# First head pair scored from unsplit float32 operands, and the planner's table retuned, in a top-k attention with a rational feed-forward

## The chip, the cores and the metric

One Trainium2 chip, one core of it. The time is device microseconds of that core for one execution; smaller is better. The engines are named as the profile names them: PE (TensorE; PEld is its weight load), DVE (VectorE), ACT (ScalarE), POOL (GpSimd) and SP (SyncE, whose queue issues every DMA of this kernel).

## The reference

```python
# attention: 8 batches, 8 heads, 576 rows, head size 64
scores = scale * np.matmul(q, k.transpose(0, 1, 3, 2))
kth = np.partition(scores, -top_k, axis=-1)[..., -top_k:-top_k + 1]     # top_k = 32
mask = scores >= kth
scores = np.where(mask, scores, -1000000000.0)
scores = scores - np.max(scores, axis=-1, keepdims=True)
attn = np.exp(scores)
attn = attn / (np.sum(attn, axis=-1, keepdims=True) + 1e-09)
attn_out = np.matmul(attn, v)
# feed-forward on x = attn_out, 4608 tokens by 512, inner size 2048
h = x @ w_in
P = a[0] + a[1] * h + a[2] * h2 + a[3] * h3                              # h2 = h*h, h3 = h2*h
Q = 1.0 + np.abs(b[0]) * np.abs(h) + np.abs(b[1]) * h2
g = P / (Q + 1e-06)
out = (g @ w_out)
```

## The kernel before, in words

**Attention.** Heads go in pairs: two heads of 64 channels fill the 128 partitions. For each batch and pair, 512 of the 576 query rows make four units of 128 rows, with one tile for each head of the pair (128 queries by 576 keys); the last 64 rows of both heads make one "mixed" tile. That is 288 tiles. A tile is scored on PE into PSUM (`scores`, L693; mixed tiles L690), copied to SBUF by ACT (`evacuate`, L700), and then DVE does the selection: it folds the two halves of 288 keys into a maximum `hi` and a minimum `lo` (L711, L704), picks eight at a time with MAX8 (L722) and MATCH_REPLACE8 (L730) until it has the 32nd largest, and multiplies mask and exponentials (`probs`, L764). ACT makes the exponentials (L761). PE turns the result (`trp`, L841), ACT copies it out (`p`, L853), PE multiplies with the values (`av`, L867). The reciprocal of the row sum is widened to 128 columns (`widen`, `rw`, on POOL L287 or ACT L285), turned by PE beside the third piece of the probabilities (L843), evacuated with it into the buffer `p2`, and multiplied into the result on POOL (`x_m`, L886).

**Split operands.** PE runs most products on fp32r operands. To keep float32 accuracy, a float32 operand is split into a high part (a copy rounded to fp32r) and a low part (the difference), and products are summed. For queries and keys that is a chain: DMA of `kl` and `qx`, a high copy (L279 on ACT or L281 on POOL), a subtraction on POOL (L592, L635), then DMAs that stack high and low parts of one head over the partitions (`ka`, `kb` L601, `q` L642 and L644). A tile then takes four fp32r matmuls of 288 columns. The mixed tiles skip all of this: they multiply float32 operands as they come (`km`), two matmuls a tile.

**Feed-forward.** A chunk of 256 tokens goes through eight groups: 24 matmuls `ph` (L1014), the rational function on ACT and POOL, and 12 matmuls `po` (L1160); chunks begin when their attention is done. Weights arrive as 64-bit floats, and 64 half-blocks are turned into float32: two operations on ACT (L416, L421), a bit merge on DVE (L427), one on ACT (L433), a product on POOL (L437), then the split (L279 or L281, L453). Before the first group, a chain of one-column operations works out the coefficients: blocks on POOL (L482, L484) with reciprocals on DVE between them (L488) and one closing operation on DVE (L552).

**Order.** Nothing is scheduled at run time. A planner (`Plan`) runs over all steps with estimated lengths, keys (smaller goes first) and rings of buffers (`ROOM`), and writes out one fixed order for each engine; on the chip an engine stops at an instruction until its semaphores are there, and all behind it waits. The dictionary `KEY` holds keys, engine choices and ring sizes; `later=` adds an estimated delay to the point at which a step may be planned. A slow full version of the program follows behind a branch and is not executed here.

Of the kernel before, what the change touches and what calls it, by code (L numbers as in the profile page):

```python
# [644 lines left out]

# [733 lines left out]
```

## Time and profile before

| | us |
|---|---|
| median of 3 runs (1514.39 to 1516.71) | 1515.34 |
| profiled execution | 1513.21 |
| its span | 1511.1 |
| PE busy in the span | 1391.7 (92%) |
| DVE busy | 1356.2 (90%) |
| ACT busy | 1270.4 (84%) |
| POOL busy | 1213.7 (80%) |

The profiled execution lies 2.1 us below the median and 2.1 us above its own span. Shares of busy time are means over stages: early on PE has little to do, and at the end DVE has nothing.

### The profile page before, as it was taken

How to read it: one execution, taken by the hardware profiler on the slowest of the kernel's cores; microseconds unless marked ns; L12 is line 12 of the kernel's file. 1: busy time of each engine (PE TensorE's matmuls, PEld its weight loads, DVE VectorE, ACT ScalarE, POOL GpSimd, SP SyncE). 2: the span in 40 equal slices, each digit the busy share in tenths (PEclk: the TensorE clock that was granted, in tenths of full speed). 3: DMA queues.
4: the chain of work that ended last, by engine and by line, in shares of the span. 5: the costliest groups of instructions: out<-in, count | busy, mean ns of one | idle time of the engine just before them, and what ended most of it. 6: DMA issues, size and time to landing. Idle time of an engine off the chain costs nothing.

```text
span 1511.1 us, 32498 instructions
## 1 busy us (share of the span) xinstructions
PE 1391.7 (92%) x9729; PEld 1174.3 (78%) x9729; DVE 1356.2 (90%) x4567; ACT 1270.4 (84%) x2512; POOL 1213.7 (80%) x1862
## 2 busy tenths in 40 slices
PE   2556789999999899999999999999999999999998
PEld 1334567878888788888888888888888788888886
DVE  5889999999999999999999999999999999999200
ACT  5768989988888788988888988888888699889774
POOL 5987898887877688887977888787878688878896
PEclk9667799999999999999999999999999999999999
DMA  8757876657765767567756776667665776564564
GB/s 240 217 176 232 236 243 207 186 158 226 231 200 153 236 200 229 176 204 214 232 175 188 221 235 202 181 189 220 207 205 156 225 208 211 157 196 148 162 203 139
DMA packets 175226, 303.21 MB, mean 201 GB/s; under 512 B 26304, under 2 KB 80576, under 8 KB 175040
## 3 DMA queue, kind: packets, MB, share of 16 engines
q1 hardware_dynamic: 175040, 301.03, 65.0%
q8 instruction: 80, 1.31, 0.4%
q14 instruction: 106, 0.87, 0.2%
HBM read 229.64 MB, written 18.87 MB: 164 GB/s over the span
## 4 chain that ended last, share of the span: by engine, by line
PE 68%; DMA 8%; POOL 6%; DVE 6%; ACT 5%; SPq 4%; issue 2%; POOLq 0%; ACTq 0%; DVEq 0%
PE ph_m L1014 19%; PE po_m L1160 18%; PE av L867 10%; PE s L693 7%; PE trp L841 7%; PE ph_t L1014 3%; DMA wi_m<-win_l 3%; PE po_t L1160 2%; DVE m L722 2%; DVE hi L730 2%; PE s L690 1%; SPq L644 1%; DMA wl_m<-wout_l 1%; DMA w_w<-in_moe_w_in_dram 1%; DVE pr L764 1%
## 5 line engine op out<-in xcount | busy, mean ns | idle before, releaser
L722 DVE MAX8 m<-hi 128x8 f32<-128x288 f32 (+1 forms) x1152 | 502.9, 455 | 0.2
L730 DVE MATCH_REPLACE8 hi<-m,hi 128x288 f32<-128x288 f32 x864 | 381.2, 446 | 0.0
L1014 PE MATMUL ph_m<-xh_m,win_h 128*128 128x256 f32 x1024 | 305.9, 299 | 2.9 <-ACT p L853 2.9
L1014 PE MATMUL ph_m<-xh_m,wi_m 128*128 128x256 f32 x1024 | 289.3, 283 | 8.3 <-DMA wi_m<-win_l 8.0
L1014 PE MATMUL ph_m<-xl_m,win_h 128*128 128x256 f32 x1024 | 288.2, 281 | 0.0
L853 ACT COPY p<-trp 128x512 f32<-128x512 f32 (+1 forms) x448 | 227.5, 513 | 37.1 <-PE trp L841 20.5
L841 PE MATMUL trp<-ident,pr 128*128 128x128 f32 x1312 | 223.2, 282 | 37.7 <-ACT w_w L433 23.5
L761 ACT ACTIVATE e<-sb,st 128x576 f32<-128x576 f32 x288 | 216.7, 752 | 26.5 <-DVE pr L764 17.1
L700 ACT COPY sb<-s 128x576 f32<-128x576 f32 x288 | 185.0, 642 | 61.2 <-PE s L693 51.0
L764 DVE SCALAR_TENSOR_TENSOR pr<-sb,m,e 128x576 f32<-128x576 f32 x288 | 230.7, 801 | 0.8 <-ACT e L761 0.7
L841 PEld LDWEIGHTS trp<-ident,pr 128*128 128x128 f32 x1312 | 163.5, 144 | 70.4 <-ACT w_w L433 28.9
L1070 POOL TENSOR_TENSOR pa_m<-pa_m,va_m 128x512 f32<-128x512 f32 x128 | 165.2, 1292 | 65.7 <-ACT va_m L1067 61.6
L1160 PE MATMUL po_m<-wout,g_m 128*128 128x512 f32 x512 | 217.5, 425 | 0.0
L1160 PE MATMUL po_m<-wl_m,g_m 128*128 128x512 f32 x512 | 203.7, 398 | 4.3 <-DMA wl_m<-wout_l 4.3
L1160 PE MATMUL po_m<-wout,gl_m 128*128 128x512 f32 x512 | 202.6, 396 | 1.1 <-DMA q<-qx 0.7
L1014 PEld LDWEIGHTS ph_m<-xh_m,wi_m 128*128 128x128 f32 x1024 | 193.2, 189 | 10.8 <-DMA wi_m<-win_l 10.7
L1014 PEld LDWEIGHTS ph_m<-xh_m,win_h 128*128 128x128 f32 x1024 | 193.5, 189 | 9.9 <-ACT p L853 4.5
L867 PE MATMUL av<-p,vm 128*64 128x256 f32 (+1 forms) x1920 | 187.6, 344 | 9.2 <-ACT w_w L433 6.0
L1014 PEld LDWEIGHTS ph_m<-xl_m,win_h 128*128 128x128 f32 x1024 | 193.6, 189 | 2.2
L1089 POOL TENSOR_TENSOR pa_m<-pa_m,hh_m 128x512 f32<-128x512 f32 x128 | 165.5, 1293 | 15.2 <-ACT hh_m L1095 5.3
L867 PEld LDWEIGHTS av<-p,vm 128*64 128x64 f32 x1920 | 111.9, 142 | 77.5 <-issue 16.0
L1076 POOL TENSOR_TENSOR gl_m<-pa_m,g_m 128x512 fp32r<-128x512 f32 x128 | 165.9, 1297 | 4.6 <-PE po_t L1160 0.2
(120 smaller groups left out, 3211.7 us busy)
## 6 DMA issues: line engine op xcount, KB each, us to landing
wl_m<-wout_l SPq DMA_DIRECT2D x256, 256.0 KB, 3.6
wi_m<-win_l SPq DMA_DIRECT2D x128, 512.0 KB, 4.2
vm<-in_v_dram SPq DMA_DIRECT2D x96, 320.0 KB, 3.2
q<-qx SPq DMA_DIRECT2D x128, 128.0 KB, 2.8
q<-qx SPq DMA_DIRECT2D x256, 64.0 KB, 2.2
km<-in_qk_dram SPq DMA_DIRECT2D x32, 352.0 KB, 3.7
kl<-in_qk_dram SPq DMA_DIRECT2D x32, 288.0 KB, 3.9
qx<-in_qk_dram SPq DMA_DIRECT2D x64, 128.0 KB, 3.5
```

Of the source, the lines that this page charges most:

```text
L700: nc.scalar.copy(t.sb, t.s[:, :, 0:HF])
L722: nc.vector.max(to, t.both if not full and o == 24 else getattr(t, src))
L730: nc.vector.match_replace(x, t.m[:, o : o + 8], x, NEG)
L761: nc.scalar.activation(t.e, t.sb, AF.Exp, scale=SCALE, bias=t.st)
L764: nc.vector.scalar_tensor_tensor(out=t.pr, in0=t.sb, scalar=t.kth, in1=t.e, op0=ALU.is_ge, op1=ALU.mult, accum_out=u.ss[:, t.h : t.h + 1],)
L841: nc.tensor.transpose(u.ps[i][:, c * P : (c + 1) * P], u.pr[:, x], ident)
L853: nc.scalar.copy(pair.pT[i][:, at].rearrange("p c n -> p (c n)"), u.ps[i][:, 0 : n * P])
L867: nc.tensor.matmul(pair.av[d, 0 : u.nq * len(pair.units)], lhs, x[:, 0, d] if u.mixed else x[:, 0] if lone else x, start=(c == 0), stop=(c ...
L1014: nc.tensor.matmul(y.ph[:, f * NT : (f + 1) * NT], w, z[:, c, :], start=(c == 0 and i == 0), stop=(c == HP - 1 and i == 2),)
L1076: engine().tensor_tensor(out=tile_("gl", F32R), in0=y.pa, in1=y.g.bitcast(F32), op=ALU.subtract)
L1089: nc.gpsimd.tensor_tensor(out=x, in0=x, in1=z, op=ALU.mult)
L1160: nc.tensor.matmul(o.po[i], z, w, start=(ff == 0 and n == 0), stop=(ff == NF - 1 and n == 2),)
```

## The change

Four things change.

1. For the first head pair of the first batch (`index == 0`), keys and queries are loaded once as float32 and multiplied as they are: one plain DMA each in place of load, split and stacking, and two float32 matmuls a tile in place of four fp32r ones, for its eight tiles. Each matmul uses the 64 partitions of its head.
2. The loads of the mixed operands of the first batch get a key that is 14 tiles later.
3. The planner takes 0.32 us in place of 0.19 us for one coefficient operation on POOL, and holds a bit merge 0.431 us longer (`ML`).
4. Entries of `KEY`: `XH` (high copies of x, keys, queries) from POOL or ACT to POOL alone; `WD` (widening) from POOL or ACT to ACT alone; `PJ` (key of `po`) 92.472 to 101.114; `RI` (key of the first denominator step) 11.198 to 7.085; rings `p2` 2 to 1, `m` 2 to 3, `ob` 3 to 4; `IL` 1.0 to 0.996, `GL` 0.3 to 0.285.

```diff
@@ -440,7 +440,7 @@

                 s1 = add("ACT", act_sb(256), sign, [ld], key + 1)
                 s2 = add("ACT", act(256, 1), ends3, [ld], key + 1, take=[bits_hold])
-                s3 = add("DVE", 0.36, merge, [s1, s2], key + 1)
+                s3 = add("DVE", 0.36, merge, [s1, s2], key + 1, later=KEY['ML'])
                 s4 = add("ACT", act_sb(256), size, [s3], key + 2, give=[bits_hold])
                 last.append(
                     add("POOL", pool_t(256), join, [s4], key + 2, give=hold if plain else [])
@@ -482,7 +482,7 @@
                         nc.gpsimd.tensor_scalar(o, x, s1, 0.0, op0=op0, op1=ALU.add)
                     else:
                         nc.gpsimd.tensor_scalar(o, x, s1, s2, op0=op0, op1=op1)
-            to("POOL", 0.19 * len(ops), emit)
+            to("POOL", 0.32 * len(ops), emit)

         def over(o, x):
             to("DVE", 0.16, lambda: nc.vector.reciprocal(o, x))
@@ -579,6 +579,11 @@
         kv.index, kv.nm = index, nm
         kv.khold, kv.mhold = Hold("k", 2 * NJ), Hold("km")
         rhold = Hold("kr")
+        kv.plain = index == 0
+
+        def load_plain():
+            kv.x = buf(kv.khold, [P, S], F32, f"ka_{nm}", "a")
+            nc.sync.dma_start(kv.x, qk[index][:, 0:S])

         def load():
             kv.low = buf(rhold, [P, S], F32, f"kl_{nm}", "l")
@@ -607,11 +612,15 @@
             kv.km, kv.qm = x[:, 0:S], x[:, S:]

         k2 = key + KEY['KL']
+        kv.mload = add("SP", dma(1, P * (S + P)), load_mixed, key=key + KEY['QL'] + (14 * T if bi == 0 else 0),
+                       take=[kv.mhold])
+        if kv.plain:
+            kv.load = add("SP", dma(1, P * S), load_plain, key=k2, take=[kv.khold])
+            return kv
         ld = add("SP", dma(1, P * S), load, key=k2, take=[rhold])
         s = add(one(S, 0, KEY['XH']), None, high_part, [ld], k2 + 1, later=KEY['LD'])
         s = add(two(S, *KEY['LP']), None, low_part, [s], k2 + 1)
         kv.load = add("SP", 4 * dma(1, D * S), stack, [s], k2 + 2, take=[kv.khold], give=[rhold])
-        kv.mload = add("SP", dma(1, P * (S + P)), load_mixed, key=key + KEY['QL'], take=[kv.mhold])
         return kv

 
@@ -622,6 +631,10 @@
         nm = f"{kv.nm}_{u.j}"
         q = pair.q = Obj()
         q.hold, rhold = Hold("q", 2 * len(pair.units)), Hold("qr")
+
+        def load_plain():
+            q.x = buf(q.hold, [P, 2, 2, 2 * P], F32, f"q_{nm}")[:, 0, 0]
+            nc.sync.dma_start(q.x[:, 0:n], qk[kv.index][:, S + u.j * P :][:, 0:n])

         def load():
             q.x = buf(rhold, [P, 2, 2 * P], F32R, f"qx_{nm}")
@@ -643,6 +656,9 @@
                 for i in range(2):
                     nc.sync.dma_start(x[there, i, h, 0:n], y[here, 1 - i, 0:n])

+        if kv.plain:
+            q.load = add("SP", dma(1, P * n), load_plain, key=key + KEY['QL'], take=[q.hold])
+            return
         ld = add("SP", dma(1, P * n), load, key=key + KEY['QL'], take=[rhold])
         s = add(one(n, 0, KEY['XH']), None, high_part, [ld], key + KEY['QL'] + 1, later=KEY['LD'])
         s = add(two(n, *KEY['LP']), None, low_part, [s], key + KEY['QL'] + 1)
@@ -683,13 +699,19 @@

         def scores():
             t.s = s = bank("s", [P, 2, 512], f"s_{t.nm}")
-            for i in range(1 if u.mixed else 2):
+            for i in range(1 if u.mixed or kv.plain else 2):
                 for hf in range(2):
                     cols = slice(hf * HF, (hf + 1) * HF)
                     if u.mixed:
                         nc.tensor.matmul(s[:, hf, 0:HF], kv.qm, kv.km[:, cols], start=True, stop=True)
                         continue
                     o = (u.j - u.pair.units[0].j) * P
+                    if kv.plain:
+                        d = slice(t.h * D, (t.h + 1) * D)
+                        nc.tensor.matmul(
+                            s[:, hf, 0:HF], u.pair.q.x[d, o : o + P], kv.x[d, cols], start=True, stop=True
+                        )
+                        continue
                     nc.tensor.matmul(
                         s[:, hf, 0:HF], u.pair.q.q[:, i, t.h, o : o + P], kv.k[t.h][:, cols],
                         start=(i == 0), stop=(i == 1),
@@ -770,8 +792,8 @@
             s = add("PE", 2 * pe_f(HF), scores, [kv.mload, prev.s], key - 3.2, take=[shold],
                     give=[kv.mhold], crit=True)
         else:
-            s = add("PE", 4 * pe_r(HF), scores, [kv.load, u.pair.q.load, prev.s], key - 3.2, take=[shold],
-                    give=[kv.khold, u.pair.q.hold], crit=True, kind="r")
+            s = add("PE", 2 * pe_f(HF) if kv.plain else 4 * pe_r(HF), scores, [kv.load, u.pair.q.load, prev.s], key - 3.2, take=[shold],
+                    give=[kv.khold, u.pair.q.hold], crit=True, kind="f" if kv.plain else "r")
         prev.s = s
         e = add("ACT", act(S), evacuate, [s], key - 2.6, take=[sbhold], give=[shold], crit=True)
         fhi = add("DVE", dve(HF), fold_hi, [e, u.fold], key - 0.6, take=[hihold] if t.h == 0 else [], give=[shold])
```

Every order is written anew by the planner. Three places of it follow; where a line's number differs between the programs, the first is before.

**SP, from the start of the program.** `km` are mixed operands, `qx` and `kl` the queries and keys to be split, `vm` values, `w_w` weight halves. Before:

```order
L606 DMA km_0_127<-in_qk_dram 128x704
L628 DMA qx_0_0_129<-in_qk_dram 128x256
L585 DMA kl_0_131<-in_qk_dram 128x576
L658 DMA vm_0_0_133<-in_v_dram 128x640
L368 DMA w_w_0_135<-in_moe_w_in_dram 128x512
L368 DMA w_w_1_137<-in_moe_w_in_dram 128x512
L606 DMA km_1_142<-in_qk_dram 128x704
L642 DMA q_0_0_146<-qx_0_0_129 64x2x256
L644 DMA q_0_0_146<-qx_0_0_129 64x256 x2
L642 DMA q_0_0_146<-qx_0_0_129 64x2x256
L644 DMA q_0_0_146<-qx_0_0_129 64x256 x2
L601 DMA ka_0_165<-kh_0_144 64x576
```

After:

```order
L637 DMA q_0_0_127<-in_qk_dram 128x256
L586 DMA ka_0_129<-in_qk_dram 128x576
L674 DMA vm_0_0_131<-in_v_dram 128x640
L368 DMA w_w_0_133<-in_moe_w_in_dram 128x512
L368 DMA w_w_1_135<-in_moe_w_in_dram 128x512
L641 DMA qx_1_0_141<-in_qk_dram 128x256
L493 DMA co<-in_moe_a_dram 128x4
L494 DMA co<-in_moe_b_dram 128x2
```

The first two DMAs are now the queries and the keys of the first pair, ready for PE; the six stacking issues of `q` and the four of `ka` and `kb` are gone from this pair, and two loads of `km` have left the start.

**ACT, behind its table load.** `sb` is the copy of a scored tile, L416, L421 and L433 work on the first weight block. Before:

```order
L416 ACTIVATE w_w_2_139<-w_w_0_135 128x256
L421 ACTIVATE w_w_b_155<-w_w_0_135,toggle 128x256
L416 ACTIVATE w_w_2_139<-w_w_1_137 128x256
L421 ACTIVATE w_w_b_159<-w_w_1_137,toggle 128x256
L433 ACTIVATE w_w_0_135<-w_w_b_155 128x256
L433 ACTIVATE w_w_1_137<-w_w_b_159 128x256
L279 ACTIVATE win_h<-w_w_2_139 128x512
L700 COPY sb_0_0_0_189<-s_0_0_0_182 128x576
L700 COPY sb_0_0_1_213<-s_0_0_1_205 128x576
```

After:

```order
L722 COPY sb_0_0_0_143<-s_0_0_0_138 128x576
L416 ACTIVATE w_w_2_137<-w_w_0_133 128x256
L421 ACTIVATE w_w_b_164<-w_w_0_133,toggle 128x256
L416 ACTIVATE w_w_2_137<-w_w_1_135 128x256
L421 ACTIVATE w_w_b_174<-w_w_1_135,toggle 128x256
L722 COPY sb_0_0_1_177<-s_0_0_1_156 128x576
L433 ACTIVATE w_w_0_133<-w_w_b_164 128x256
L783 ACTIVATE e_0_0_0_185<-sb_0_0_0_143,st_0_0_154 128x2x288
L433 ACTIVATE w_w_1_135<-w_w_b_174 128x256
```

The first tile's copy now stands ahead of the first weight block, and the second tile's copy (`sb_0_0_1`) stands behind L416 and L421 of both of its halves.

**DVE, around the closing operation of the coefficient chain (L552), in the fourth head pair of the first batch.** Before:

```order
L711 TENSOR_TENSOR hi_0_3_1013<-s_0_3_0_950,sb_0_3_0_972 128x288
L722 MAX m_1_2_881<-hi_1_2_860 128x8
L704 TENSOR_TENSOR lo_0_3_0_1032<-s_0_3_0_950,sb_0_3_0_972 128x288
L730 MATCH_REPLACE hi_1_2_860<-m_1_2_881,hi_1_2_860 128x288
L427 SCALAR_TENSOR_TENSOR w_w_b_1034<-w_w_0_662,w_w_b_1034 128x256
L722 MAX m_1_2_881<-hi_1_2_860 128x8
L722 MAX m_0_3_1048<-hi_0_3_1013 128x8
L764 SCALAR_TENSOR_TENSOR pr_1_2_907,ss_1_2_908<-sb_1_2_1_899,m_1_2_881,e_1_2_1_986 128x576
L552 TENSOR_TENSOR cf<-cf 128x1
L730 MATCH_REPLACE hi_0_3_1013<-m_0_3_1048,hi_0_3_1013 128x288
```

After:

```order
L733 TENSOR_TENSOR hi_0_3_988<-s_0_3_1_1008,sb_0_3_1_1020 128x288
L744 MAX m_0_3_1003<-hi_0_3_988 128x8
L726 TENSOR_TENSOR lo_0_3_1_1058<-s_0_3_1_1008,sb_0_3_1_1020 128x288
L752 MATCH_REPLACE hi_0_3_988<-m_0_3_1003,hi_0_3_988 128x288
L744 MAX m_0_3_1003<-hi_0_3_988 128x8 x2
L752 MATCH_REPLACE hi_0_3_988<-m_0_3_1003,hi_0_3_988 128x288
L786 SCALAR_TENSOR_TENSOR pr_0_3_1067,ss_0_3_1068<-sb_0_3_0_977,m_0_3_1003,e_0_3_0_1069 128x576
L744 MAX hi_0_3_988<-lo_0_3_1_1058 128x8
L744 MAX m_0_3_1003<-hi_0_3_988 128x8
L427 SCALAR_TENSOR_TENSOR w_w_b_1056<-w_w_0_950,w_w_b_1056 128x256
L752 MATCH_REPLACE hi_0_3_988<-m_0_3_1003,hi_0_3_988 128x288
L552 TENSOR_TENSOR cf<-cf 128x1
```

L552 stood behind the first pick of that pair's first tile and now stands in its second tile. Counted in rows of DVE's order, the chain from its first reciprocal to L552 held 117 other operations and now holds 128. On PE the first `ph` stands behind the scores of tile 23 in both programs, and when the last tile is scored 4557 of the 5184 feed-forward matmuls stood ahead of it before and 4554 after.

## Rows read from the trace of the kernel before

**Rows 1.** Windows: busy time of PE, PEld, DVE, ACT, POOL; granted clock, DMA.

```profile
...
40.00:100.00 60.00, 29.50 (x120) 18.82 (x118) 50.54 (x169) 42.39 (x102) 55.24 (x119) 0.62 0.69 209
100.00:150.00 50.00, 35.13 (x228) 24.54 (x228) 45.27 (x151) 40.20 (x101) 35.02 (x63) 0.74 0.66 211
150.00:250.00 100.00, 79.16 (x498) 60.70 (x497) 97.04 (x324) 89.09 (x194) 88.64 (x139) 0.88 0.76 233
250.00:1400.00 1150.00, 1131.92 (x8203) 969.69 (x8201) 1132.72 (x3825) 1005.17 (x1947) 923.28 (x1406) 1.00 0.65 199
1400.00:1500.00 100.00, 100.00 (x632) 88.83 (x632) 6.30 (x22) 69.25 (x114) 88.04 (x89) 1.00 0.57 180
...
```

**Rows 2.** Timeline of the start, all engines: start, length, engine, line, operation.

```profile
...
1.19 0.42 SPq L628 DMA_DIRECT2D qx<-in_qk_dram  x1
...
4.42 0.41 POOL L281 TENSOR_SCALAR qx<-qx 128x256 fp32r<-128x256 f32 x1 [3.04 <-DMA qx<-in_qk_dram]
...
6.36 1.40 POOL L592 TENSOR_TENSOR kl<-kl,kh 128x576 fp32r<-128x576 f32 x1
...
8.96 0.43 DVE L427 SCALAR_TENSOR_TENSOR w_w_b<-w_w,w_w_b 128x256 int32<-128x256 int32 x1 [8.96 <-ACT w_w_b L421]
...
10.60 0.43 DVE L427 SCALAR_TENSOR_TENSOR w_w_b<-w_w,w_w_b 128x256 int32<-128x256 int32 x1 [1.21 <-ACT w_w_b L421]
...
12.31 0.60 SPq L601 DMA_DIRECT2D kb<-kh  x1
...
13.68 1.30 PE L693 MATMUL s<-ka,q 128*128 128x288 f32 x4 [13.68 <-DMA ka<-kl]
...
15.69 0.46 DVE L711 TENSOR_TENSOR hi<-s,sb 128x288 f32<-128x288 f32 x1 [4.67 <-ACT sb L700]
...
```

**Rows 3.** DMA issues, first 16 us: count, KB each, median us to landing.

```profile
...
kl<-in_qk_dram SPq DMA_DIRECT2D x2, 288.0 KB, 4.6
...
qx<-in_qk_dram SPq DMA_DIRECT2D x2, 128.0 KB, 2.7
...
```

**Rows 4.** Timeline of PE near 100 us: split and unsplit scores.

```profile
...
98.28 1.31 PE L693 MATMUL s<-ka,q 128*128 128x288 f32 x4
...
110.25 2.00 PE L690 MATMUL s<-km 128*128 128x288 f32 x4
...
```

**Rows 5.** DVE's waits, 40 to 250 us: total us, times, longest.

```profile
...
DVE w_w_b L427 <- ACT w_w_b L421: 8.3, 13, 1.0
DVE cf L488 <- POOL cf L484: 4.7, 4, 1.4
DVE cf L552 <- POOL cf L484: 1.7, 1, 1.7
...
```

**Rows 6.** Timeline of DVE: first reciprocal of the chain, and its closing operation.

```profile
...
27.11 0.15 DVE L488 RECIPROCAL cf<-cf 128x1 f32<-128x1 f32 x1
...
91.89 1.20 DVE L552 TENSOR_TENSOR cf<-cf 128x1 f32<-128x1 f32 x1 [1.71 <-POOL cf L484]
...
```

**Rows 7.** Groups by line: busy us, mean ns of one, idle before.

```profile
...
L287 POOL TENSOR_SCALAR rw<-ss 128x128 f32<-128x128 f32 x93 | 28.1, 302 | 10.2 <-DVE ss L819 8.7 <-PE po_t L1160 0.5 <-PE po_m L1160 0.3
...
L285 ACT ACTIVATE rw<-ss 128x128 f32<-128x128 f32 x67 | 21.1, 315 | 0.3 <-DVE ss L819 0.2
...
L279 ACT ACTIVATE xh_m<-x_m 128x512 fp32r<-128x512 f32 x15 | 9.5, 634 | 5.5 <-PE ph_m L1014 5.2 <-PE ph_t L1014 0.3
...
```

**Rows 8.** DVE's waits, 250 to 1407 us.

```profile
...
DVE hi L711 <- ACT sb L700: 12.7, 19, 1.4
...
```

**Rows 9.** Timeline: product `x_m` on POOL, next third copy on ACT.

```profile
...
309.19 0.74 POOL L886 TENSOR_TENSOR x_m<-x_m,p 128x256 f32<-128x256 f32 x1
...
314.83 0.35 ACT L853 COPY p<-trp 128x256 f32<-128x256 f32 x1
...
740.40 0.74 POOL L886 TENSOR_TENSOR x_m<-x_m,p 128x256 f32<-128x256 f32 x1
740.99 0.37 ACT L853 COPY p<-trp 128x256 f32<-128x256 f32 x1
...
1361.91 0.74 POOL L886 TENSOR_TENSOR x_m<-x_m,p 128x256 f32<-128x256 f32 x1
...
1365.52 0.40 ACT L853 COPY p<-trp 128x256 f32<-128x256 f32 x1
...
```

**Rows 10.** Timeline of DVE at the end of attention.

```profile
...
1405.23 0.81 DVE L764 SCALAR_TENSOR_TENSOR pr<-sb,m,e 128x576 f32<-128x576 f32 x1
...
```

More of the change, by code (lines that the diff above doesn't have):

```diff
@@ L19 @@
 PSUM = bass.MemoryType.PSUM
-KEY = {'STAY': 0.0, 'WH': ('ACT', 'POOL'), 'XH': ('POOL', 'ACT'), 'TH': 0, 'EU': 4.119, 'SC': 0, 'HW': 256, 'Q0': ('POOL', 'ACT'), 'Q1': ('POOL',), 'SPLIT': (0, 1, 2, 3, 4, 5, 6, 7), 'XS': 1, 'P1': ('ACT', 'POOL'), 'P3': ('ACT', 'POOL'), 'RH': ('POOL',), 'p2': ('POOL', 'DVE'), 'p4': ('POOL',), 'ratio': ('POOL', 'DVE'), 'ratio_low': ('POOL',), 'URG': -100.0, 'PT': -10.303, 'AV': 2.038, 'MOE': 125.127, 'QT': -12.596, 'KT': -22.066, 'EL': 1.0, 'LOOK': 0.27, 'T': 5.448, 'KL': -16.348, 'KH': -8.844, 'PJ': 92.472, 'WL': 0.96, 'EX': 8.711, 'EW': 9.121, 'ALT': {'ACT': 0.388, 'DVE': 29.071, 'POOL': 0}, 'WG': 5.531, 'QL': -17.951, 'QH': 0.956, 'PACE': 15.382, 'B4': 0, 'RT': 1.0, 'WI': 0, 'WO': 0, 'MS': 0.313, 'NM': ('POOL', 'ACT'), 'WD': ('POOL', 'ACT'), 'LP': ('POOL',), 'FL': ('DVE',), 'VL': -15.549, 'RI': 11.198, 'ROOM': {'s': 1, 'e': 1, 'mm': 2, 'o': 2, 'k': 4, 'kr': 1, 'km': 2, 'q': 2, 'qr': 1, 'v': 2, 'sb': 3, 'lo': 1, 'hi': 2, 'pr': 2, 'p0': 1, 'p1': 1, 'p2': 2, 'm': 2, 'u': 4, 'rw': 1, 'fl': 2, 'x': 2, 'xm': 1, 'xs': 1, 't': 14, 'ob': 3, 'wi': 2, 'wl': 4}, 'TN': 2, 'IL': 1.0, 'SLACK': {'DVE': 0.0, 'PE': 0.0, 'ACT': 0.0, 'POOL': 0.0}, 'CF': 5.0, 'LD': 1.5, 'CL': 1.0, 'C0': 6.0, 'GL': 0.3}
@@ new lines @@
+KEY = {'STAY': 0.0, 'WH': ('ACT', 'POOL'), 'XH': ('POOL',), 'TH': 0, 'EU': 4.119, 'SC': 0, 'HW': 256, 'Q0': ('POOL', 'ACT'), 'Q1': ('POOL',), 'SPLIT': (0, 1, 2, 3, 4, 5, 6, 7), 'XS': 1, 'P1': ('ACT', 'POOL'), 'P3': ('ACT', 'POOL'), 'RH': ('POOL',), 'p2': ('POOL', 'DVE'), 'p4': ('POOL',), 'ratio': ('POOL', 'DVE'), 'ratio_low': ('POOL',), 'URG': -100.0, 'PT': -10.303, 'AV': 2.038, 'MOE': 125.127, 'QT': -12.596, 'KT': -22.066, 'EL': 1.0, 'LOOK': 0.27, 'T': 5.448, 'KL': -16.348, 'KH': -8.844, 'PJ': 101.114, 'WL': 0.96, 'EX': 8.711, 'EW': 9.121, 'ALT': {'ACT': 0.388, 'DVE': 29.071, 'POOL': 0}, 'WG': 5.531, 'QL': -17.951, 'QH': 0.956, 'PACE': 15.382, 'B4': 0, 'RT': 1.0, 'WI': 0, 'WO': 0, 'MS': 0.313, 'NM': ('POOL', 'ACT'), 'WD': ('ACT',), 'LP': ('POOL',), 'FL': ('DVE',), 'VL': -15.549, 'RI': 7.085, 'ROOM': {'s': 1, 'e': 1, 'mm': 2, 'o': 2, 'k': 4, 'kr': 1, 'km': 2, 'q': 2, 'qr': 1, 'v': 2, 'sb': 3, 'lo': 1, 'hi': 2, 'pr': 2, 'p0': 1, 'p1': 1, 'p2': 1, 'm': 3, 'u': 4, 'rw': 1, 'fl': 2, 'x': 2, 'xm': 1, 'xs': 1, 't': 14, 'ob': 4, 'wi': 2, 'wl': 4}, 'TN': 2, 'IL': 0.996, 'SLACK': {'DVE': 0.0, 'PE': 0.0, 'ACT': 0.0, 'POOL': 0.0}, 'CF': 5.0, 'LD': 1.5, 'CL': 1.0, 'C0': 6.0, 'ML': 0.431, 'GL': 0.285}
```

## The prediction

> **What bounds the kernel now.** I read the busy shares of the page first, then busy time by stage, because a mean over the span mixes three limits. In [rows 1] the reader should subtract busy time from the length of each window. From 250 to 1400 us DVE is idle for 17.3 of 1150 us and PE for 18.1: both are full, and since each follows a fixed order the two go in step. From 40 to 150 us DVE is busy for 95.8 of 110 us and PE for 64.6: there attention, DVE's work, sets the pace, and PE waits for it. Attention ends at about 1406 [rows 10]. Behind it DVE is idle and PE works without a gap at one matmul per 0.16 us (100 us, 632 matmuls, rows 1) until just past 1500: that is the feed-forward left over when attention ends.
>
> So the end is the end of attention plus the left-over PE work. The order lists show the left-over as 627 matmuls before and 630 after, and the first `ph` behind the same tile. A microsecond that DVE gains before PE fills up at about 250 us therefore moves everything behind it, PE too: PE's early idle time, not its work, shrinks.
>
> Where can DVE gain? The timeline of the start [rows 2] shows that the first attention operation of DVE stands at 15.69 us, 2.0 us behind the first score matmul at 13.68, which waited for the last stacking DMAs. The waits [rows 5] show 6.4 us behind POOL's coefficient blocks and 8.3 us in 13 waits for ACT ahead of bit merges.
>
> **The start.** The chain DMA, high copy, subtraction, stacking of queries and keys goes. What stays is one load each, the keys issued second, at the time that the `qx` issue has now, 1.19 us. The landing of an unhindered key load at that place is not in the trace. Bounds: `qx` took 2.7 us for 128 KB, `kl` 4.6 us for 288 KB behind 480 KB of other loads [rows 3], so 3.9 to 5.8 us. I take 4.8, nearer to the row of the same size but with less ahead of it. PE needs a price for two unsplit matmuls with 64 partitions; the mixed tiles are the nearest rows: four of them (two tiles) took 2.00 us, and four split ones, one tile, 1.31 us not far from it [rows 4], the same as the 1.30 us at 13.68 [rows 2]. Both stand where the granted clock is low, a mean of 0.62 and 0.74 of full speed in their windows [rows 1]. So a first tile takes about 1.1 us, 0.2 less than now. From PE's start to DVE's start it is then 1.8 us: DVE begins at 6.6 in place of 15.69, **9.1 us earlier** (bounds 7.9 and 10.0). The seven other plain tiles gain as little each, and DVE has other work in that time: counted as nothing; without that cover they would be worth 7 times 0.2, 1.4 us.
>
> Against it: DVE did the first two bit merges, 0.43 us each, while it waited for the first scores [rows 2]. Now they stand between attention operations: **+0.9**. On ACT the copy of the second tile now stands behind both halves of the first weight block, so it waits for the second half to land, and DVE's second merge waits with it. Its wait was 1.2 us [rows 2]; fewer loads go ahead of it now, and DVE has other work until about 9.8 us. I take **+0.5** (0 to 1.2).
>
> The keys of the second pair still go through splitting and stacking, behind POOL and, on SP's queue, behind two stores of weight parts. DVE asks for them some 21 us after its start, as before, and the issues of the first pair that stood ahead of them are gone, so I price that at nothing. If they were late, DVE would stop for them once.
>
> **The coefficient chain.** From the first reciprocal at 27.1 to the closing operation at 91.9 there are 64.8 us [rows 6], with 117 other DVE operations and 6.4 us of waits for POOL [rows 5]; with about 3 us of other waits taken off, one operation is worth 0.47 us. Now 128 operations stand in the same chain. If POOL's pace stays, 11 more operations cover 5.2 us of the waits: **-5.2** (0 if POOL falls back by as much, -6.4 if all go). POOL is busy for 55.2 of the 60 us from 40 to 100 [rows 1], so this term depends on it. In its favour, the four split operations of the first pair, 4.42 to 7.76 us [rows 2], go.
>
> **The merges.** A hold of 0.431 us can take at most that from each of 13 waits, 5.6 us. I take two thirds, **-3.7**, because ACT's and POOL's later steps on the same weights move back as well (0 to -5.6).
>
> **The left-over.** Three more matmuls at 0.16 us: **+0.5**.
>
> **The middle.** 93 widenings of 0.302 us leave POOL and cost ACT 0.315 each, and high copies go the other way, 0.634 us each for those of x [rows 7]. By the counts of the order lists ACT gains some 14 us and POOL loses some 16. ACT is busy for 87% from 250 to 1400 [rows 1], and what reaches DVE from it is 12.7 us in 19 waits for `sb` [rows 8]. The later `po` key and the earlier denominator step shift matmuls and ACT operations by a few places, while the count of feed-forward matmuls ahead of a tile stays within 33 of the old one throughout (some 5 us of PE). I take nothing; the bounds are -12.7, all those waits, and the price of the slower rival below.
>
> The ring `p2` of one buffer is the edit with a danger. The third evacuation of the next head pair (ACT) must now wait until `x_m` of the pair before has read the buffer. How far the two lie apart can be read now: in 51 pairs between 309 and 1366 us the gap is 4.9 us at the first and 2.9 at the last shown, and least at 740, where the copy starts 0.15 us before the product ends [rows 9]. Only that one would collide at today's places. So: nothing.
>
> **Sum.** -9.1 + 0.9 + 0.5 - 5.2 - 3.7 + 0.5 = -16.1 us on the profiled execution of 1513.2, which gives 1497.1. The median of the runs is 2.1 above that execution, so 1499.2: I say **1499**.
>
> **A rule weighed against the rows.** The two kinds of score in [rows 4] put the unsplit tile at some 1.0 to 1.1 us against 1.3 for the split one. The Trainium skill, FP8 and Floating Point Precision, section Matmul Precision, states that true FP32 takes four passes through the array. By that rule two unsplit matmuls would be as long as eight split ones, and the trace does not agree: they took half a microsecond each, less than twice a split one. It is the last rival below.
>
> **The rivals.**
> - *Only the head start counts.* The waits for POOL and ACT form again further on, since both work in order on the same weights. For it: POOL at 92% in that stretch. Against it: 11 more operations of cover. -9.1 + 0.9 + 0.5 + 0.5 = -7.2: 1508.
> - *The middle gains too.* Shorter steps on POOL and a denominator that starts earlier take half of the 12.7 us of `sb` waits: 1493. Against it: those waits begin at PE, which is full.
> - *POOL holds the start.* The first weight products cannot begin before the weights land, so the chain's end moves only by the 3.3 us of split work that POOL loses, and DVE waits for the rest: 1512, half of it within 0.2%.
> - *Slower: the single `p2` buffer.* If `x_m` came later against the next third copy than now, ACT would stop in front of that copy, with the copies of scores and the exponentials for DVE behind it. Summed over the 51 gaps, 2 us later costs ACT 11.9 us, 3 us later 25.9. It decides from about 2.3 us, where it eats the 16 us if ACT's spare 13% takes none of it. At 3 us: 1499 + 26 = 1525. For it: 64 pairs of full units now share one buffer. Against it: POOL has less to do than before.
> - *Unsplit matmuls cost four split ones.* The first tile would take 2.6 us, not 1.1, and the start lose 1.5: 1500.7.
>
> **How the numbers follow.** Forecast 57% (its own range 1494 to 1505), head start only 15%, middle too 10%, POOL 8%, single buffer 8%, four passes 2%. The range 1490 to 1510 holds the first three and the last, and leaves out POOL's and the buffer's cases. A change of 0.2%, 3 us, is about what a measurement of this kernel can tell from none. Faster: 57 + 15 + 10 + 2 and half of POOL's 8, 88%, of which I give 1% away for what I have not seen: 87. Same: 4 and that 1, 5. Slower: 8.
>
> **What the next profile would show.** Right: the first score of PE at 4 to 6 us, DVE's first attention operation at 6 to 8; the waits of L488 and L552 under 2 us together; merge waits from 40 us on under 6; attention ending near 1390 and PE full behind it for the same 100 us. Wrong: a wait of `hi` for `sb` of several microseconds at the second or the fifth tile; waits of the third copy for `x_m`; PE idle between 250 and 1400 by more than 18 us; attention that ends early with a longer PE stretch behind it.

## The result, and the profile after

| | before | after |
|---|---|---|
| median of 4 runs each (us) | 1514.87 | 1499.43 |
| lowest and highest | 1513.32, 1516.71 | 1497.78, 1500.79 |
| profiled execution, its span | 1513.21, 1511.1 | 1500.79, 1498.9 |
| start of the last `probs` of DVE | 1405.23 | 1391.16 |
| from there to the end of the span | 105.9 | 107.7 |

The ratio is 0.9897 (0.988 to 0.9914): 15.4 us by the medians, 12.4 by the two profiled executions, since before's lies 0.1 us below its four runs and after's is its slowest. What follows is about the 12.4 unless it says medians.

Busy time by window in after, the same columns as [rows 1]; the last two windows end and begin where attention now ends:

```profile
40.00:100.00 60.00, 32.35 (x134) 21.11 (x133) 56.18 (x186) 47.80 (x119) 55.19 (x109) 0.61 0.70 219
100.00:150.00 50.00, 37.42 (x200) 24.62 (x198) 43.63 (x144) 36.12 (x92) 36.21 (x63) 0.64 0.72 219
150.00:250.00 100.00, 81.73 (x580) 64.39 (x578) 97.42 (x325) 91.72 (x208) 87.21 (x129) 0.95 0.75 231
250.00:1390.00 1140.00, 1125.15 (x8139) 966.38 (x8136) 1125.86 (x3801) 1003.16 (x1992) 906.35 (x1335) 1.00 0.65 199
1390.00:1490.00 100.00, 99.88 (x617) 87.84 (x616) 2.30 (x9) 66.52 (x109) 87.42 (x88) 1.00 0.55 177
```

Against [rows 1], from 40 to 100 us DVE is busy for 56.2 us where it was busy for 50.5. From 100 to 150 us it is the other way round: 43.6 against 45.3. PE is busier there (37.4 against 35.1) at a lower granted clock (0.64 against 0.74). Behind attention PE is as full as before.

The start of after, all engines (against [rows 2] and [rows 3]), and the end of attention (against [rows 10]):

```profile
0.74 0.40 SPq L637 DMA_DIRECT2D q<-in_qk_dram  x1
1.19 0.42 SPq L586 DMA_DIRECT2D ka<-in_qk_dram  x1
...
4.48 2.26 PE L711 MATMUL s<-ka,q 64*128 64x288 f32 x4 [4.48 <-DMA ka<-in_qk_dram]
...
7.45 0.46 DVE L733 TENSOR_TENSOR hi<-s,sb 128x288 f32<-128x288 f32 x1 [7.45 <-ACT sb L722]
...
9.84 0.41 DVE L427 SCALAR_TENSOR_TENSOR w_w_b<-w_w,w_w_b 128x256 int32<-128x256 int32 x1
10.59 0.42 DVE L427 SCALAR_TENSOR_TENSOR w_w_b<-w_w,w_w_b 128x256 int32<-128x256 int32 x1
...
1391.16 0.81 DVE L786 SCALAR_TENSOR_TENSOR pr<-sb,m,e 128x576 f32<-128x576 f32 x1
```

The first attention operation stands at 7.45, 8.24 us earlier, and the two merges have no wait in front of them. The keys landed at 4.48. But the first tile takes PE 2.26 us, where the split tile of before took 1.30 [rows 2].

Scores of PE in after, groups of lines with the shapes apart: records, then busy us and mean ns of one record.

```profile
L706 PE MATMUL s<-km 128*128 128x288 f32 x128 | 40.5, 442 | 2.1 <-DVE lo L726 2.0
L711 PE MATMUL s<-ka,q 64*128 64x288 f32 x32 | 17.0, 681 | 11.7 <-DVE lo L726 7.1 <-DMA ka<-in_qk_dram 4.5
```

The eight unsplit tiles have 32 records and the 32 mixed tiles 128. A tile has two float32 matmuls, so one such matmul leaves two records, and "x4" is one tile, not two.

DVE's waits in after from 40 to 250 us (against [rows 5]) and from 250 to 1395 (against [rows 8]): us in total, times, longest.

```profile
DVE hi L733 <- ACT sb L722: 5.9, 6, 2.0
DVE w_w_b L427 <- ACT w_w_b L421: 3.7, 5, 1.4
DVE ss L841 <- POOL ss L281: 1.7, 1, 1.7
DVE cf L552 <- POOL cf L484: 0.7, 1, 0.7
...
DVE cf L488 <- POOL cf L484: 0.3, 1, 0.3
...
DVE hi L733 <- ACT sb L722: 10.3, 13, 2.4
```

The waits for POOL's coefficients fell from 6.4 to 1.0 us and those for merges from 8.3 to 3.7. Waits of `hi` for scores, 1.2 us before in that stretch, are now 5.9.

**The course of the lead.** How far each kernel is from the kernel before at the start of `probs` of a tile (us, minus is earlier; the 288 starts are read from the timelines of DVE). The `_wl_last`, `_fill` and `_warm` kernels are experiments told below.

| tile | 1 | 17 | 25 | 41 | 97 | 105 | 193 | 288 |
|---|---|---|---|---|---|---|---|---|
| time in before | 22.10 | 121.95 | 166.40 | 252.41 | 509.79 | 546.52 | 959.16 | 1405.23 |
| after | -8.8 | -15.5 | -9.3 | -9.3 | -12.2 | -8.2 | -7.8 | -14.1 |
| plain_alone | -8.2 | -8.6 | -4.6 | -5.4 | 1.3 | 5.3 | 9.1 | 7.8 |
| plain_fill | -6.8 | -8.4 | -4.9 | -5.8 | -3.8 | -1.0 | -1.2 | -2.9 |
| chain_alone | -0.6 | -7.9 | -8.6 | -9.5 | -2.2 | 4.3 | 5.6 | -0.1 |
| chain_wl_last | -0.2 | -8.3 | -9.4 | -6.8 | -4.5 | -2.8 | -6.1 | -12.8 |
| before_wl_last | 0.0 | -0.5 | 0.7 | 1.1 | -0.4 | -0.4 | -4.5 | -11.2 |
| after_wl_last | -9.0 | -17.1 | -11.7 | -10.0 | -13.5 | -13.5 | -16.6 | -21.8 |
| after_wl_warm | -9.2 | -16.9 | -6.0 | 0.5 | -3.0 | -3.1 | -6.8 | -13.3 |

plain_alone and plain_fill have one order up to tile 43 and differ by 1.4 us at tile 1: that much is the scatter of single executions.

So by tile 17 the change has gained 15.5 us, near what the sum gave for the end. It gives 6.2 us back by tile 25, loses 4.0 from tile 97 to 105, and wins 6.3 between tiles 193 and 288, where nothing was forecast. The experiments are about these three.

Windows of 4 us about the loss at 490 in after:

```profile
490.00:494.00 4.00, 1.58 (x11) 1.16 (x9) 4.00 (x13) 2.50 (x7) 1.58 (x5) 1.00 0.87 241
494.00:498.00 4.00, 3.25 (x15) 3.25 (x16) 4.00 (x15) 1.10 (x3) 2.25 (x4) 0.50 0.99 331
498.00:502.00 4.00, 4.00 (x25) 3.70 (x26) 1.65 (x7) 1.62 (x5) 0.00 (x0) 0.65 0.29 111
502.00:506.00 4.00, 4.00 (x36) 3.18 (x33) 4.00 (x13) 4.00 (x9) 3.21 (x6) 1.00 0.65 197
```

PE in the same place, timeline:

```profile
491.61 0.28 PE L1036 MATMUL ph_m<-xl_m,win_h 128*128 128x256 f32 x1
494.75 0.58 PE L1036 MATMUL ph_m<-xh_m,wi_m 128*128 128x256 f32 x1 [2.86 <-DMA wi_m<-win_l]
495.13 0.41 PE L1036 MATMUL ph_m<-xh_m,win_h 128*128 128x256 f32 x1
```

Read them together. PE is busy for 1.58 of 4 us and then waits 2.86 us for the low weights (`wi_m`) of a group. Right behind that the granted clock is 0.50, 1.2 GHz, and records of 0.28 us become 0.41. PE is then full, and DVE, short of scores, is busy for 1.65 of 4 us. In before the same place has a wait of 1.84 for `wi_m` with the clock at 1.00, and DVE stays full:

```profile
505.93 0.39 PE L1014 MATMUL ph_m<-xh_m,wi_m 128*128 128x256 f32 x1 [1.84 <-DMA wi_m<-win_l]
...
502.00:506.00 4.00, 1.52 (x12) 1.11 (x9) 4.00 (x15) 2.08 (x5) 1.44 (x4) 1.00 0.92 265
506.00:510.00 4.00, 4.00 (x32) 3.76 (x32) 4.00 (x15) 2.43 (x5) 2.74 (x5) 1.00 0.99 333
```

### The profile page after: what moved, and what is told of

It reads as the page before. It is cut to its first block, busy times and chain, and to the rows that moved or that the text cites. A ratio compares the mean times of both kernels' runs of the same rounds, so it can differ in the third digit from the quotient of the medians.

```text
span 1498.9 us, 32412 instructions
## 1 busy us (share of the span) xinstructions
PE 1400.6 (93%) x9729; PEld 1178.6 (79%) x9729; DVE 1356.2 (90%) x4567; ACT 1274.5 (85%) x2592; POOL 1197.0 (80%) x1776
## 4 chain that ended last, share of the span: by engine, by line
PE 74%; DVE 8%; ACT 6%; POOL 5%; issue 3%; DMA 2%; SPq 1%; POOLq 0%; ACTq 0%; DVEq 0%
PE ph_m L1036 21%; PE po_m L1182 19%; PE av L889 10%; PE s L715 8%; PE trp L863 7%; PE ph_t L1036 3%; DVE m L744 3%; PE po_t L1182 2%; DVE hi L752 2%; PE s L706 2%; DVE pr L786 1%; DMA wi_m<-win_l 1%; ACT p L875 1%; ACT sb L722 1%; PE trp L865 1%
## 5 line engine op out<-in xcount | busy, mean ns | idle before, releaser
L783 ACT ACTIVATE e<-sb,st 128x576 f32<-128x576 f32 x288 | 216.8, 753 | 18.9 <-DVE pr L786 15.4
```

The source lines that it names most:

```text
L783: nc.scalar.activation(t.e, t.sb, AF.Exp, scale=SCALE, bias=t.st)
```

## The experiments

| kernel | median us | ratio to before | last `probs` | from there to the end | feed-forward matmuls left |
|---|---|---|---|---|---|
| plain_alone | 1522.89 | 1.0054 (1.0035 to 1.0073) | 1413.04 | 111.2 | 651 |
| chain_alone | 1520.88 | 1.0054 (1.0037 to 1.0072) | 1405.11 | 112.0 | 654 |
| table_alone | 1524.64 | 1.0066 (1.0041 to 1.0092) | 1408.51 | 115.1 | 690 |
| no_plain | 1509.75 | 0.9971 (0.9953 to 0.9989) | 1392.67 | 116.2 | 669 |
| after_wl_last | 1491.57 | 0.9852 (0.9831 to 0.9874) | 1383.38 | 107.5 | 630 |
| before_wl_last | 1501.10 | 0.9918 (0.9895 to 0.9941) | 1393.99 | 104.6 | 627 |
| chain_wl_last | 1506.32 | 0.9951 (0.9929 to 0.9973) | 1392.45 | 111.0 | 654 |
| plain_fill | 1514.95 | 1.0013 (0.9997 to 1.0029) | 1402.34 | 110.7 | 651 |
| after_wl_warm | 1502.04 | 0.9932 (0.9913 to 0.9951) | 1391.91 | 107.2 | 630 |
| table_wl_last | 1513.99 | 1.0010 (0.9997 to 1.0024) | 1395.06 | 115.1 | 690 |
| no_plain_wl_last | 1504.47 | 0.9942 (0.9925 to 0.9960) | 1388.24 | 115.6 | 669 |
| no_chain_wl_last | 1510.99 | 0.9991 (0.9973 to 1.0009) | 1392.22 | 115.7 | 669 |

Measured beside these kernels, before had a median of 1513.3 us each time. The last column counts in PE's order what stands behind the last scores; before it is 627, after 630.

**One part alone, and all but one.** plain_alone has only the unsplit first pair, chain_alone only the 0.32 us and the hold of the merges, table_alone only the entries of the table; no_plain is after without the unsplit pair. The later loads of the mixed operands are in no_plain, in after and in what is made from these two, and were not tried alone.

no_plain against after (chain_alone and table_alone have this line too):

```diff
-        kv.plain = index == 0
+        kv.plain = False
```

plain_alone and table_alone against after, with `ML` at 0 and, in plain_alone and chain_alone, the table's entries as before:

```diff
-            to("POOL", 0.32 * len(ops), emit)
+            to("POOL", 0.19 * len(ops), emit)
```

- plain_alone: 

> The kernel before with the unsplit first pair alone; table, chain lengths, merge hold and the load key of the mixed operands as before. Theory A (each part gives what the trace shows for it): DVE's first attention operation at 7.5 us as after the whole change, 8.2 us earlier, less 0.9 for two merges that now stand in the way, so 7 to 8 us off 1514.9: 1507 +- 2; the waits of L488 and L552 for POOL stay near 6 us. Rival B (POOL's pace holds the start): the head start is eaten by longer waits of L488 and L552, 10 us or more, and the time is 1512 or above.


- chain_alone: 

> The kernel before with the longer coefficient lengths (0.32 us) and the merge hold (0.431 us) alone. Theory A: the waits of L488 and L552 fall from 6.4 us to about 1, those of merges between 40 and 250 us from 8.3 to about 4, and 8 to 10 us come off: 1505 to 1507. Rival B (the waits only change places): as many microseconds come back as waits of hi for sb, and less than 4 us come off: 1511 or above.


- table_alone: 

> The kernel before with the retuned entries of KEY alone (XH, WD, PJ, RI, rings, IL, GL). Theory A: the middle gains nothing, 1515 +- 3. Rival B (the retuned table is where the time came from): 1507 or less, with less waiting of DVE behind 250 us.


- no_plain: 

> The changed kernel with the first pair split again (mixed loads stay late). Theory A: DVE begins at about 15 us again, the end moves back by 7 to 8 us: 1507 +- 2. Rival B (POOL's pace holds the start): within 3 us of the changed kernel, 1502 or less.

Each part alone is slower than before; three expectations missed by 10 to 16 us, and no_plain by 3. The early gains are there all the same: 8.2 us at tile 1 in plain_alone, 7.9 at tile 17 in chain_alone. They are lost later, between tiles 41 and 105 (10.7 and 13.8 us), and the order left 24 to 63 more matmuls to the end. So the parts act early as forecast, and do not add up in the end. Chain_alone shows what the loss looks like:

```profile
252.00:256.00 4.00, 2.18 (x14) 1.41 (x12) 4.00 (x16) 3.44 (x7) 3.58 (x7) 1.00 0.91 250
256.00:260.00 4.00, 1.61 (x7) 1.61 (x8) 4.00 (x16) 1.27 (x3) 3.36 (x7) 0.50 0.87 336
260.00:264.00 4.00, 4.00 (x25) 4.00 (x24) 2.31 (x8) 1.45 (x3) 0.08 (x1) 0.65 0.01 6
```

Again PE is half idle, then slow at 0.50, then full while DVE starves. Two readings were open: the falls of the clock cost the time, or the written order does.

**The low weights last.** In a `ph` group the products that read the loaded low weights go behind the 16 that do not. The planner's order is the same.

```diff
...
-                for i, (w, z) in enumerate(((wh, o.xh), (wh, o.xl), (wl, o.xh))):
+                work = [(n, d, i) for n in range(FG) for d in range(HP) for i in range(2)]
+                work += [(n, d, 2) for n in range(FG) for d in range(HP)]
+                at = 3 * (f * HP + c)
+                for n, d, i in work[at : at + 3]:
...
```

- after_wl_last: 

> The changed kernel in the same order, only with the products of each ph group that read the loaded low weights (wi) put behind all those that do not, so that 16 matmuls of about 0.115 us lie ahead of the first that needs the load. Clock theory: of the four waits for wi (6.3 us, longest 2.9 at 494) less than 2 us stay, the granted clock no longer falls to 0.50 at 494 to 500, and the 4 us that DVE lost there (tiles 97 to 105) come back: 1495.5. Rival, the pause has nothing to do with the clock: the clock falls all the same at 490 to 500, and the time stays at 1499 within 1.5.


- before_wl_last: 

> The same edit in the kernel before, whose eight waits for wi (8.0 us, longest 1.8) came with no fall of the granted clock. Clock theory: nothing to get back, since DVE set the pace around them: 1514, at most 2 us lower. Rival, each pause of PE is lost by itself: 8.0 less what stays, 1508.


- chain_wl_last: 

> The same edit in the kernel with only the retuned chain and merge lengths (1520.9), where PE waits for wi by 3.5 us at 258 and 2.9 at 527 and the granted clock falls to 0.5 to 0.6 near both. Clock theory: the first fall goes and with it some 4 of the 8.3 us that DVE loses in tiles 40 to 48, and of the 7.6 us in tiles 96 to 112 those behind 527, some 3: 1514. Rival, the order itself is what makes that kernel slow: 1519 to 1521.

Windows of after_wl_last at the place where after had lost 4.0 us:

```profile
490.00:494.00 4.00, 2.83 (x25) 2.65 (x24) 4.00 (x15) 2.39 (x5) 1.76 (x6) 1.00 0.96 315
494.00:498.00 4.00, 3.90 (x34) 3.01 (x34) 4.00 (x16) 3.24 (x7) 3.28 (x5) 1.00 0.97 334
498.00:502.00 4.00, 3.68 (x31) 3.26 (x28) 4.00 (x14) 3.94 (x9) 2.06 (x5) 1.00 0.68 212
```

The clock stays at 1.00, DVE stays full, and the lead at tiles 97 and 105 is 13.5 both times. The median is 7.9 us below that of after, more than the 3.9 expected; before itself lay 1.6 us lower beside this kernel than beside after, so 6.3 of it is the kernel's own.

before_wl_last contradicts the clock theory as I had put it: at most 2 us were to be had, and 12.2 came (1513.3 to 1501.1). The largest PE wait of before in 250 to 1400 us and DVE's wait behind it:

```profile
PE ph_m L1014 <- DMA wi_m<-win_l: 8.0, 8, 1.8
...
DVE hi L711 <- ACT sb L700: 12.7, 19, 1.4
```

The same two views of before_wl_last, where waits for `wi_m` are gone:

```profile
PE po_m L1164 <- DMA wl_m<-wout_l: 4.0, 3, 1.7
...
DVE hi L711 <- ACT sb L700: 2.1, 6, 0.4
```

So in the middle, where both engines are full, a pause of PE returns as a wait of DVE even at a clock of 1.00: with the 8.0 us of waits for weights 10.6 of the 12.7 us of `sb` waits went, and attention ends 11.2 us earlier. The rival (each pause is lost) is right here; by it alone 1508 was expected, so 1501 is more than the pauses themselves. Part of the rest is a fall of the clock that before has and before_wl_last has not: 0.83 at 1180 to 1190 us. Between tiles 225 and 257, which hold it, the lead grows by 3.4 us. In before a wait of 2.2 us for `wl_m`, the low weights of `po`, stands ahead of that fall.

chain_wl_last lost 1.7 us from tile 97 to 105 where chain_alone lost 6.5, and ended 14.6 us lower, 8 us below the 1514 of the theory. From tile 41 on it still lost some 2 us to tile 97, and its clock still fell to 0.80 to 0.86 from 210 to 250 us, where PE waits for ACT and not for a load (2.2 us at 216, 2.0 at 240), and to 0.63 from 500 to 510.

**Pauses filled with work that nobody reads.** That separates the clock from the waiting, since PE gains no time. In plain_alone, ahead of three sets of transposes:

```diff
+                if not full and (u.nm, i) in (("1_1_0", 0), ("1_1_0", 1), ("2_3_0", 0)):
+                    for _ in range(16):
+                        nc.tensor.matmul(
+                            u.ps[i][:, 0:NT], win_h[:, 0, 0:P], win_h[:, 0, 0:NT], start=True, stop=True
+                        )
```

> The kernel with only the unsplit first pair (1522.9), with 16 matmuls of 256 columns that nobody reads put ahead of three sets of transposes: the two of the second unit of the first full head pair of the second batch (PE waited there for 0.6 and 2.2 us at 257 and 262) and the first of a unit of the third batch (2.2 us at 507). They add 48 matmuls of 0.115 us, 5.5 us of PE's time, to places where it waited 5.0. Clock theory: the granted clock does not fall at 256 to 268 and 508 to 516, and DVE gets back some 4 us in tiles 40 to 48 and 5 in tiles 96 to 112: 1514. Rival, pauses do not decide the clock, so this is work added: 1523 to 1526.

Windows of plain_alone:

```profile
256.00:260.00 4.00, 1.87 (x9) 1.12 (x9) 4.00 (x15) 4.00 (x9) 3.92 (x6) 0.93 0.68 201
260.00:264.00 4.00, 1.52 (x6) 1.25 (x6) 4.00 (x12) 3.65 (x8) 3.84 (x7) 0.50 0.86 314
264.00:268.00 4.00, 3.71 (x17) 3.71 (x18) 3.69 (x15) 0.91 (x2) 4.00 (x6) 0.50 0.02 9
```

The same windows of plain_fill:

```profile
256.00:260.00 4.00, 3.35 (x25) 3.04 (x25) 4.00 (x15) 3.17 (x7) 3.92 (x5) 1.00 0.76 233
260.00:264.00 4.00, 3.51 (x27) 3.20 (x27) 4.00 (x15) 3.97 (x9) 3.84 (x7) 1.00 0.72 255
264.00:268.00 4.00, 4.00 (x36) 3.33 (x36) 4.00 (x14) 2.23 (x4) 4.00 (x6) 1.00 0.03 6
```

With 48 useless matmuls more the kernel is 7.9 us faster (1514.95; expected 1514). The clock holds at 1.00 and DVE is full in all three windows, and between tiles 43 and 52, right behind, the kernel gains 2.9 us on plain_alone. At this place it is shown, not argued, that the clock falls by the pause and that the fall costs DVE time. The Trainium skill, TensorE: Matmul & The Clock Gate, Part 1, says that the gate lets through half or all of the pulses by how busy PE has been, and these rows agree.

The total came out as expected partly by other places. At the third set the clock still fell, to 0.74 from 506 to 510 us, and from tile 97 to 113 only 1.1 us came where 5 were expected. Another 3.3 of the 10.7 us at the end of attention come between tiles 118 and 124, at 628 us, where no filler stands: there plain_alone waits 2.5 us for `wi_m` and its clock falls, and plain_fill waits 0.7 us.

**The same idea at 110 to 165 us**, where 6.2 us are given back: after_wl_last with 8 such matmuls ahead of both main sets of transposes of the units of tiles 14 to 31.

```diff
+                if not full and i < 2 and 14 <= u.tiles[0].n < 32:
+                    for _ in range(8):
...
```

> after_wl_last (1491.6) with 8 matmuls of 256 columns that nobody reads ahead of the first two sets of transposes of each unit of tiles 14 to 31, where the granted clock is 0.5 to 0.88 and PE busy for 6 to 7 of 10 us, and where the kernel falls from 17.1 to 11.7 us ahead of the kernel before (tiles 19 to 24). Clock theory: the clock in 100 to 160 us rises above 0.8, DVE waits less there, and half of the 5.4 us stays: 1489. Rival, PE's speed is not what DVE waits for there, and the fillers stand ahead of scores: 1493 to 1497, with DVE later by tile 32.

A miss: 1502.04, the rival's direction and more (1493 to 1497 was its price). First after_wl_last, which the fillers were added to, then after_wl_warm:

```profile
100.00:150.00 50.00, 36.54 (x203) 24.25 (x201) 43.31 (x144) 37.45 (x96) 34.85 (x63) 0.67 0.73 225
150.00:250.00 100.00, 84.19 (x573) 65.88 (x574) 97.22 (x325) 90.05 (x203) 87.63 (x128) 0.92 0.74 226
```

```profile
100.00:150.00 50.00, 38.19 (x241) 28.20 (x240) 39.33 (x128) 33.89 (x89) 32.94 (x59) 0.75 0.61 186
150.00:250.00 100.00, 83.38 (x578) 67.41 (x579) 91.40 (x305) 85.24 (x190) 79.53 (x117) 0.97 0.73 224
```

The clock rose, from 0.67 to 0.75 and from 0.92 to 0.97, and DVE did 4.0 and 5.8 us less. Its waits for ACT ahead of merges went from 4.2 to 11.0 us in these 150 us. So the higher clock did not pay here: the fillers, which stand ahead of transposes that ACT copies out, cost more than it gave.

What DVE waits for in the give-back can be read without an experiment. From `probs` of tile 17 to that of tile 25 it runs 142 instructions of the same kinds in before and in after, but is idle for 2.0 us in before (121.9 to 166.4 us) and for 7.4 in after (106.5 to 157.1). Its waits there, before and then after:

```profile
DVE w_w_b L427 <- ACT w_w_b L421: 0.8, 2, 0.6
```

```profile
DVE w_w_b L427 <- ACT w_w_b L421: 3.4, 4, 1.4
DVE ss L841 <- POOL ss L281: 1.7, 1, 1.7
DVE hi L733 <- ACT sb L722: 1.3, 1, 1.3
```

The other four unsplit tiles are scored just here, at 121 to 140 us, in 1.20, 2.25, 2.25 and 2.29 us. ACT and DVE behind the last one, in after:

```profile
137.93 2.29 PE L711 MATMUL s<-ka,q 64*128 64x288 f32 x4
...
140.25 0.64 ACT L722 COPY sb<-s 128x576 f32<-128x576 f32 x1 [2.04 <-PE s L711]
...
140.92 0.46 DVE L733 TENSOR_TENSOR hi<-s,sb 128x288 f32<-128x288 f32 x1 [1.32 <-ACT sb L722]
```

So the price of an unsplit tile reaches DVE here: a split one would have ended some 1 us sooner at the same clock, an estimate from the 2.26 and 1.30 us of the first tiles. How much of the 6.2 us this makes was not tried: no kernel was run with only the second four split.

**The parts again, with the low weights last.** The same edit in table_alone, in no_plain, and in after with 0.19 us and no hold (no_chain_wl_last).

- table_wl_last: 

> The kernel with only the retuned entries of the table (1524.6), with the late use of the low weights. Its order leaves 690 feed-forward matmuls behind the last scores where the kernel before leaves 627. Theory that the left-over makes it slow: 63 times 0.16, 10 us, above the kernel before with the same late use (1501.1): 1511. Rival, it was slow by its waits for wi and the clock: 1501 to 1503.


- no_plain_wl_last: 

> The changed kernel without the unsplit first pair (1509.8), with the late use of the low weights. Left-over 669 matmuls against 630. Theory: against after_wl_last (1491.6) it lacks the head start (6 to 7 us, curves at tile 1) and has 39 times 0.16, 6.2 us, more left over: 1504. Rival, only the head start: 1498.


- no_chain_wl_last: 

> The changed kernel with 0.19 us for a coefficient operation and no hold of the merges, with the late use of the low weights. Left-over 669 matmuls against 630. Theory: against after_wl_last (1491.6) it lacks the 8 us that the chain and the merges gave by tile 16 and has 6.2 us more left over: 1506. Rival, the chain's gain is given back by tile 24 whatever is done, so only the left-over tells: 1498.

The left-over theory holds roughly, worst for the last: 1513.99 for 1511 expected, 1504.47 for 1504, 1510.99 for 1506. The stretch behind the last `probs` is 115.1 to 115.7 us in these three, against 104.6 and 107.5 in before_wl_last and after_wl_last. That is 8.1 and 8.2 us for 39 matmuls and 10.5 for 63, 0.17 to 0.21 us each, a little above the 0.16 that I reckoned with. The count alone does not settle it, since 690 left matmuls took no longer than 669. So what one part is worth depends on the others, in part through how much feed-forward the written order leaves to the end: with the low weights last, the unsplit pair is worth 12.9 us on top of the other two (1504.47 to 1491.57), the chain and merge lengths 19.4 (1510.99 to 1491.57), while the latter alone cost 5.2 (1501.10 to 1506.32). Why the planner leaves so much more in some combinations was not tried.

## Why the prediction was right, and what was wrong inside it

The forecast was 1499 us, the median 1499.43. On the profiled execution -16.1 was forecast and -12.4 came. The sum came out by terms that were right early and by two errors, of 6.2 and 4.8 us, in opposite directions. That these nearly cancel is luck, as neither was forecast. With the low weights last on both sides the change is worth 9.5 us by the medians (1501.10 to 1491.57), not 15.4: part of the hit hung on where each order happens to wait for a load.

- **The start**, -9.1: measured -8.24. (By its own terms the lower bound is 8.1, not 7.9: 15.69 less 5.8 and 1.8.) Landing was right (4.48 for 4.8). The price of an unsplit tile was wrong by a factor of two: I read the four records of [rows 4] as two tiles at 1.0 to 1.1 us, but they are one tile of 2.00. At the low clock it is 2.26 us, dearer than the split tile's 1.30. So the seven other plain tiles cost PE up to 1 us more each, not 0.2 less. I counted them as nothing because DVE has other work in that time; for the last of them that was wrong, since DVE waited 1.32 us behind it. The Trainium skill, FP8 and Floating Point Precision, Matmul Precision, with its four passes gives 2.6 us for the tile by the split row; the measured 2.26 lies far nearer to it than my 1.1. From record to record the trace agrees: at the low clock the records of an unsplit tile start 0.48 us apart and those of a split one 0.24, and a float32 matmul has two. I gave that rival 2 in 100 on a misread row. Its price for the start, 1.5 us, was near the 0.86 that came.
- **Merges on the path**, +0.9: measured 0.83. **The second merge's wait**, +0.5: none.
- **The chain**, -5.2: waits fell by 5.4. **The later merges**, -3.7: waits fell by 4.6. At tile 17 the lead is 15.5 us where these terms gave 16.6. Counted by what came before tile 17, it is -8.24 and +0.83 for the start, -5.4 for the chain, -4.8 for merges and +2.5 for new waits for `sb`: -15.1.
- **What failed** is the step "A microsecond that DVE gains before PE fills up at about 250 us therefore moves everything behind it". From tile 17 to 25, 6.2 us went, 5.4 of them as waits of DVE, most of all for merges. PE is not yet full there (busy for 37.0 of 50.6 us at a clock of 0.67; before, for 29.6 of 44.5 at 0.73), so the lead was lost ahead of the point that I had named. The give-back is there with the low weights last too (17.1 to 11.7), so it is not the wait for `wi`. In no_plain_wl_last the lead at tiles 17, 25 and 27 is 12.4, 9.0 and 12.3, and chain_alone, without the unsplit pair too, loses nothing there. Then the unsplit pair adds 4.7 at tile 17, 2.7 at 25 and nothing at 27 (17.1, 11.7 and 11.8 in after_wl_last). To that extent the rivals by which the gain does not last were right, though it is not shown to be POOL that takes it. The length of the second four unsplit tiles and the lower clock are the candidates; which of them it is stays open.
- **The middle**, 0: right as to the change itself. With the low weights last on both sides, the lead of after over before is 12.4 us at tile 25, 13.1 at 97 and 10.6 at 288. Between the two kernels as they are, it moved from 9.3 to 14.1, since each has its own waits for `wi_m`: after 6.3 us in 4, before 8.0 in 8. My reading that the 12.7 us of `sb` waits [rows 8] begin at a full PE was wrong in a way that counts: of the 18.1 idle us of PE that I named, 8.0 were waits for a load, and their removal took 10.6 of those 12.7. Of the engines, POOL lost 16.7 us of work, as reckoned, and ACT gained 4.1, not 14.
- **The left-over**, +0.5: the stretch behind attention grew by 1.8.
- **The single `p2` buffer**, nothing: no wait of ACT's third copy for `x_m` shows in after's waits. Twice that copy waited for the product of a mixed tile (`xm`, L920), which reads the same buffer: 0.34 us at 242 and 1.26 at 255. The slower rival did not occur.
- Of the signs that were to show it right, merge waits under 6 us and coefficient waits under 2 came true, as did attention's end near 1390. PE idle from 250 to 1390 is 14.9 us, under the 18. The sign for wrong, waits of `hi` for `sb`, came in part: 5.9 us from 40 to 250.

By the curve of the lead: -15.5 to tile 17, +6.2 to tile 25, +1.1 to tile 105, -5.9 to the last, +1.8 behind it, -12.3 in all, the spans' 12.2.

## What to carry to other kernels

A small idle time of a nearly full engine deserves its own list of waits: 8 us of PE waiting for a load in 1150 were worth 12 us, some 3 of them where a fall of the clock went too, and the remedy was to put the products that need the load last in their group. After a change of order compare the starts of the same step all along, not only the ends: gains, give-backs and falls of the clock are then seen where they happen. A written order's parts cannot be priced one by one; count what each order leaves to the end.

## What the runs showed of the hardware

In the middle of a kernel whose PE is 98% busy, pauses of PE were followed by a granted clock of 0.50 (494 us in after, 256 in chain_alone, 260 in plain_alone), and matmuls that nobody reads, put in place of such pauses, held the clock at 1.00 from 256 to 268 us and gained 2.9 us there. Not every pause was followed by it: behind that of 1.84 us in before the clock stood at 1.00. Where PE was busy for 36.5 of 50 us at a clock of 0.67, fillers raised the clock to 0.75 and cost 10.5 us. A float32 matmul stands in the trace as two records. At a mean clock of 1.00 (300 to 1380 us of after) the unsplit mixed tile takes 28.0 us for 24 tiles, 1.17 each, and the split one 152.9 for 207, 0.74.
